# Placing the global keys and queries of a Longformer batch one batch sooner on GpSimd, with the keys in eight copies

## The chip, the core and the metric

The kernel runs on one core of one Trainium2 chip. The metric is the device time of one execution in microseconds (us), lower is better. Times are given as the median of several runs, and one further execution was profiled instruction by instruction. The engines are called PE (TensorE matmul), PEld (its weight load), DVE (VectorE), ACT (ScalarE), POOL (GpSimd) and SP (SyncE, which here only issues DMAs). L12 stands for line 12 of the kernel.

## What is computed

The reference is a Longformer attention, followed by a two-layer block with the activation h + sin²(αh)/α. There are 8 batches, 8 heads, 576 positions and a head size of 64. A position attends to positions at most 32 away, and 8 global positions attend to all and are attended by all:

```python
mask = np.abs(pos[:, None] - pos[None, :]) <= window
mask = mask | is_global[:, None] | is_global[None, :]
attn = softmax(where(mask, q @ k.T / sqrt(D), -1e9))
x = (attn @ v)                       # (8, 8, 576, 64) -> 4608 x 512
h = x @ w_in                         # 512 x 2048
out = (h + sin(alpha * h) ** 2 / (alpha + 1e-9)) @ w_out
```

## The kernel before

**Stages.** Batches are taken one after the other. For each batch b there is an attention stage (`attention`, L712) and then `gemm1(b)` (L947), which computes 16 column tiles of h and applies the activation. `gemm2`, the second product, has no stage of its own: its matmuls (L1033) are dealt out as filler between those of the other stages by `fill`, in numbers that tables at L1076 to L1082 set by hand. The outer loop at L1131 runs `gemm1(b)` and then `phase_a(b + 1, b)`, the attention of the next batch. The schedule is manual: every engine executes its instructions in the order in which the program lists them, and the framework only adds the semaphores that the data need.

**Attention.** Heads are taken in four pairs. For a pair, PE multiplies keys by queries into a PSUM ring (L736, three groups of four key tiles), ACT takes the exponential (L744), DVE multiplies by the mask (L747), and PE multiplies the result by V and by ones (L778, `products`). ACT then makes the inverse of the sums (L804, L807), and DVE the sums over global columns (L788) and the normalised x (L810). The products of a pair are issued behind the first two score groups of the next pair.

**The placed operands.** Keys, queries and V of a batch lie in the tiles `KX`, `QX` and `VX`, each of them twice (index b % 2). In every key tile of 128 partitions and 128 columns, a part holds the 48 keys of a window, and the 8 columns behind them hold the global keys; the same global keys stand in all 12 key tiles of a pair. A batch is brought in by four routes:

- `cast_qk` (L323) casts q and k to bf16 through two DMAs of POOL's queue; `turn_qk` (L333) turns them with two transposing DMAs on SP's queue, after `gemm1` of the batch two before; `place` (L342) copies them into KX and QX on DVE (lines L354 and L347), spread over the attention stage before, or over the end of gemm1(0) and gemm1(1) for batches 1 and 2.
- `load_v` (L385) brings V into VX by four DMAs of POOL's queue for each pair of heads (L390). A pair's DMAs wait until the products of the same pair, two batches before, have read VX.
- `load_vg` (L395) brings V's global rows by eight DMAs of SP's queue (L399).
- `place_globals` (L364) copies the global keys (L368) and queries (L373) into KX and QX on POOL, from the small tiles `kTg` and `qTg`, which hold those of all batches from gemm1(0) on.

**The order on POOL's queue.** At the top of the loop, for b from 1 to 5, POOL gets the casts for b + 2, V's pair 0 for b + 2, `place_globals(b + 1)`, V's pairs 1 to 3 for b + 2, and nothing else until the next b. For b = 6 it gets only `place_globals(7)`. Batch 1's placement is issued inside gemm1(0) (L997). Since V for b + 2 waits for the products of batch b, most of that list runs during attention(b).

**gemm1.** Each of the 16 column tiles takes eight matmuls (L972) into one of three PSUM tiles, zn, zr and zd in turn. ACT takes the sine (L1009), ACT (L1013) or DVE (L1015) the square, and DVE adds the parts (L1020), which frees the PSUM tile. In attention, DVE and ACT also work on a check of the inputs' ranges (`square_x`, L896 to L901, and `square_w`, L870 and L872), which decides at the end whether a general path must run.

The lines of POOL's list in the loop are these:

```python
            cast_qk(b + 2)
            load_v(b + 2, (0,))

            place_globals(b + 1)
            load_v(b + 2, range(1, NHP))
            load_vg(b + 2)
```

Of the kernel before, what the change touches and what calls it, by code (L numbers as in the profile page):

```python
# [18 lines left out]
NG = 8  # L19
KT = 48  # L20
# [227 lines left out]
def kernel(  # L248
# [11 lines left out]
    nc = tc.nc  # L260
    B, H, S, D = q.shape
# [3 lines left out]
    NT12 = S // KT  # L265
    NHP = H // 2
# [27 lines left out]
    KX = [main.tile([P, NHP, NT12, P], DT.bfloat16, name=f"KX{i}") for i in range(2)]  # L294
# [8 lines left out]
    kTg = main.tile([P, NHP, NG, B], DT.bfloat16, name="kTg")  # L303
# [19 lines left out]
    def cast_qk(b):  # L323

        cast[b] = []
        for src, name in ((k, "kd"), (q, "qd")):
            t = dramp.tile([P, H * S * D // P], DT.bfloat16, name=name)
            nc.gpsimd.dma_start(
                out=t[:], in_=src[b].rearrange("h s d -> (h s d)").rearrange("(p f) -> p f", p=P)
            )  # L330
            cast[b].insert(0, t)

    def turn_qk(b):  # L333

        turned[b] = [trp.tile([P, H * HALF], DT.bfloat16, name=name) for name in ("qt", "kt")]
        for i in (1, 0):
            nc.sync.dma_start_transpose(
                out=turned[b][i][:], in_=cast[b][i][:].rearrange("p (r c) -> (p r) c", c=P)
            )
        del cast[b]  # L340
# [22 lines left out]

    def place_globals(b):  # L364

        for t in range(2):
            rows = slice(t * D, (t + 1) * D)
            nc.gpsimd.tensor_copy(  # L368
                out=KX[b % 2][rows, :, :, t * D + KT : t * D + KT + NG],
                in_=kTg[rows, :, None, :, b].to_broadcast([D, NHP, NT12, NG]),  # L370
            )
        for y in range(2):
            nc.gpsimd.tensor_copy(  # L373
                out=globals_of(b, slice(0, P), y),
                in_=qTg[:, :, None, y::2, b].to_broadcast([P, NHP, 7, 4]),
            )

    def globals_of(b, rows, y):

        q0 = QX[b % 2][rows, :, y, PAD : PAD + 4]  # L380
        return bass.AP(
            tensor=q0.tensor, offset=q0.offset, ap=[list(q0.ap[0]), [2 * QROW, NHP], [SEG, 7], [1, 4]]
        )

    def load_v(b, hps=range(NHP)):  # L385
        for hp in hps:
            for t in range(2):
                for y in range(2):
                    r = t * D + y * 24
                    nc.gpsimd.dma_start(  # L390
                        out=VX[b % 2][r : r + 24, hp, :, t * D : t * D + D],
                        in_=v[b, 2 * hp + t].rearrange("(i a y) d -> y a i d", a=24, y=2)[y],
                    )

    def load_vg(b):  # L395
        for h in range(H):
            t = h % 2
            src = VGb[b::B, h * D : (h + 1) * D] if b else VG0[h::H]
            nc.sync.dma_start(  # L399
                out=VX[b % 2][t * D + KT : t * D + KT + NG, h // 2, :, t * D : t * D + D],  # L400
                in_=src[:, None, :].to_broadcast([NG, NT12, D]),
            )
# [35 lines left out]
    for half in range(2):  # L438
        for w, src in ((1, k), (0, q)):
            nc.gpsimd.dma_start(  # L440
                out=nat[w][D * half : D * half + HK],
                in_=src[0, HH * half : HH * half + HH].rearrange("h (i r) d -> (h i) (r d)", r=KT),
# [22 lines left out]
    for t in (gidx8, gp64):  # L465
        nc.vector.memset(t[:].bitcast(DT.int32), 0)
    nc.sync.dma_start(
        out=g64[:],
        in_=bass.AP(tensor=global_idx.tensor, offset=global_idx.offset, ap=[[1, NG], [0, B], [1, 1]]),
# [3 lines left out]
    for t in (0, D):  # L473
        nc.sync.dma_start(out=gp64[t + KT : t + KT + NG], in_=global_idx[:, None])
        nc.sync.dma_start(
            out=gidx8[t + KT : t + KT + NG],
            in_=bass.AP(tensor=global_idx.tensor, offset=global_idx.offset, ap=[[0, NG], [1, NG]]),
# [29 lines left out]
    for i, bits in enumerate((B - 1, D - 1)):  # L507
        nc.vector.tensor_scalar(
            out=rowi[:, i : i + 1], in0=prow[:], scalar1=bits, scalar2=None, op0=ALU.bitwise_and
# [6 lines left out]
        out=cond[:, 0:1], in0=pm, scalar1=float(NH), scalar2=float(1 - KT), op0=ALU.is_ge, op1=ALU.mult  # L516
# [3 lines left out]
        out=kpos[:], in0=pm, scalar=2.0, in1=cond[:, 0:1], op0=ALU.mult, op1=ALU.add  # L520
    )
    nc.vector.scalar_tensor_tensor(
        out=kpos[:], in0=cond[:, 1:2], scalar=float(4095 + KT), in1=kpos[:], op0=ALU.mult, op1=ALU.add
# [4 lines left out]
        out=rowf[0 : NG * B, 4:5], in0=rowf[0 : NG * B, 0:1], scalar=float(S), in1=rowf[0 : NG * B, 3:4], op0=ALU.mult, op1=ALU.add  # L528
# [19 lines left out]
    for name, src in (("k", k), ("q", q), ("v", v)):  # L548
        g0[name] = VG0 if name == "v" else setup.tile([NG * B, D], DT.bfloat16, name="g0" + name)
        nc.gpsimd.indirect_dma_start(  # L550
            out=g0[name][:], out_offset=None, in_=src[0].rearrange("h s d -> (h s) d"),
# [16 lines left out]
        out=band[:], in0=qrel[:], scalar1=float(WIN * WIN) + 0.5, scalar2=None, op0=ALU.is_le  # L568
    )
    for t in (0, D):  # L570
# [4 lines left out]
        out=M2, in_=band[:].rearrange("p e x c -> p e (x c)")[:, None].to_broadcast([P, 6, 2, WCOL])  # L575
# [49 lines left out]
    def place_global_queries(t, copy):  # L625
# [15 lines left out]
        out=first[:], in0=gf[:], scalar1=gpf[:, 0:1], scalar2=None, op0=ALU.not_equal  # L641
# [3 lines left out]
        out=later[:], in0=jrow[:], scalar1=pm, scalar2=float(-KT), op0=ALU.subtract, op1=ALU.is_ge  # L645
# [5 lines left out]
        out=cond[:, 2:3], in0=pm, scalar=float(KT + NG - 1), in1=cond[:, 1:2], op0=ALU.is_le, op1=ALU.mult  # L651
# [5 lines left out]
        out=far[:], in0=qpos[:], scalar1=float(WIN * WIN) + 0.5,  # L657
# [13 lines left out]
    for w, name in ((1, "k"), (0, "q")):  # L671
        pg[w] = both[0:D, 32 + w * 64 : 64 + w * 64].bitcast(DT.bfloat16)
        nc.tensor.transpose(
            out=pg[w][:], in_=g0[name][:], identity=identb[0 : NG * B, 0 : NG * B]
# [272 lines left out]
    def gemm1(b):  # L947
# [35 lines left out]
        for nt in range(NT):  # L983
# [9 lines left out]
            if b == 0 and nt == 11:  # L993

                load_w_out()
                cast_globals_v()
                place_globals(1)  # L997
                load_v(1, (2, 3))
                load_vg(1)
# [91 lines left out]
    def phase_a(b_att, b_moe):  # L1091
        def beside(at):

            if b_moe is None:
                if at == -1:
                    nc.vector.tensor_scalar(out=recipT[:], in0=alphaT[:], scalar1=1e-9, scalar2=None, op0=ALU.add)
                    nc.vector.reciprocal(out=recipT[:], in_=recipT[:])
                if at == 0:
                    second_half()
                    nc.gpsimd.memset(VX[1][:].bitcast(DT.int32), 0)  # L1100
                    nc.gpsimd.memset(QX[1][:].bitcast(DT.int32), 0)
                    nc.gpsimd.memset(KX[1][:].bitcast(DT.int32), 0)
                    turn_qk(1)
                    nc.gpsimd.tensor_copy(out=seen[:], in_=turned[1][1][0:1, 0:1])
                    load_w_in((2, 3))
                    load_v(1, (0, 1))
                    gather(v, gv)
                return
            if at == 0:
                if b_moe == 2:  # L1110
                    column_norms(zn[:, 0, :])
                if b_moe >= 3:
                    token_norms(b_moe - 3, zn[:, 1, :])
            if 0 <= at < 2 and b_moe:
                square_x(b_moe, at)
            if b_att == 1 and at == 0:
                place_rest(1)
                place_rest(0)
            for which, t, y in places_at(b_att, at):
                place(b_att + 1, which, t, y, nc.vector.tensor_copy)  # L1120
            if b_moe == 0 and at == 2:
                turn_qk(2)
            if b_moe == 1 and at in (2, 3):
                square_w(at)

        if b_moe is not None:
            waiting.append(gemm2(b_moe))
        attention(b_att, beside)

    phase_a(0, None)  # L1130
    for b in range(B):  # L1131
        if 0 < b and b + 2 < B:
            cast_qk(b + 2)
            load_v(b + 2, (0,))

            place_globals(b + 1)
            load_v(b + 2, range(1, NHP))
            load_vg(b + 2)
        elif 0 < b < B - 1:
            place_globals(b + 1)  # L1140
        gemm1(b)
        if b + 1 < B:
            if b == 0:
                cast_qk(2)
                load_v(2)
                load_vg(2)
            elif b + 2 < B:
                turn_qk(b + 2)
            phase_a(b + 1, b)
# [46 lines left out]
```

## Time and profile before

| What | us |
|---|---|
| median of 3 runs | 382.2 (379.91 to 382.34) |
| the profiled execution | 381.18 |
| its span, first to last instruction | 379.5 |
| PE, DVE, ACT, POOL busy in it | 342.2, 288.4, 294.3, 133.8 |

The stages follow each other in the profile like this, by the first score matmul and the first gemm1 matmul of each batch:

| batch | attention from | gemm1 from |
|---|---|---|
| 0 | 15.5 | 33.0 |
| 1 | 54.1 | 72.3 |
| 2 | 99.6 | 120.1 |
| 3 | 142.2 | 162.3 |
| 4 | 182.6 | 202.6 |
| 5 | 222.9 | 243.0 |
| 6 | 263.2 | 282.0 |
| 7 | 302.4 | 321.2 |

POOL ran `place_globals` seven times. Its key copies start at 51.1, 86.6, 109.5, 152.5, 192.7, 233.2 and 246.7 us. A line of the profile's order of time gives the start, the time from first to last instruction of a run of equal ones, engine, line, operation, the tiles written and read, the shapes, the number of instructions, and in brackets how long the engine had stood idle before it and what ended that. A line of the wait list gives who waited for whom, the microseconds in total, and how often.

### The profile page before, as it was taken

What the parts mean: (1) busy time and instruction counts of PE and PEld (TensorE: products, weight loads), DVE (VectorE), ACT (ScalarE), POOL (GpSimd) and SP (SyncE); (2) the same over time, 40 slices, a digit from 0 to 9 for tenths busy, and PEclk for the clock granted to TensorE, in tenths of its full rate; (3) what the DMA queues carried; (4) which work ended last, traced back from release to release, by engine and by line L of the source; (5) the groups of instructions that cost most, each with busy time, mean ns of one, the idle gap of its engine ahead of it and who ended that gap; (6) DMA issues with size and microseconds to landing.
All of it is one profiled execution on the core that took longest, in us unless ns stands there. A gap on an engine that the chain in (4) does not pass through costs nothing. (4 is left out here: it accounts for less than half of the span.)

```text
span 379.5 us, 8635 instructions
## 1 busy us (share of the span) xinstructions
PE 342.2 (90%) x3172; PEld 233.3 (61%) x3172; DVE 288.4 (76%) x614; ACT 294.3 (78%) x566; POOL 133.8 (35%) x204
## 2 busy tenths in 40 slices
PE   2679869997998899999989999999999998999893
PEld 2567646764565666676656766666676666776341
DVE  6777897589889887988888888888788876589400
ACT  7789897898889788788878887889888888675111
POOL 7993695559477101840086006720000000000001
PEclk9999999999999999999999999999999999999998
DMA  6999999999999863789069923727111011100221
GB/s 119 119 161 186 155 153 174 147 173 179 182 181 119 137 114 74 91 99 216 28 81 94 204 62 45 75 40 155 42 44 29 0 41 46 29 3 28 57 85 48
DMA packets 103579, 38.08 MB, mean 100 GB/s; under 512 B 94138, under 2 KB 98250, under 8 KB 103082
## 3 DMA queue, kind: packets, MB, share of 16 engines
q0 software_dynamic: 56640, 18.56, 42.4%
q1 hardware_dynamic: 46890, 18.89, 25.1%
q8 instruction: 27, 0.44, 0.5%
q14 instruction: 22, 0.18, 0.1%
HBM read 37.15 MB, written 17.83 MB: 145 GB/s over the span
## 5 line engine op out<-in xcount | busy, mean ns | idle before, releaser
L1033 PE MATMUL zo<-w_out,H 128*128 128x512 bf16 x576 | 153.2, 378 | 0.0
L972 PEld LDWEIGHTS <-w_in 128*128 128x128 bf16 x1024 | 99.2, 97 | 48.4 <-issue 14.8
L390 POOL DMA_DIRECT2D VX<-in_v_dram x128 | 83.7, 663 | 105.7 <-PE zd L778 87.4
L1033 PEld LDWEIGHTS <-H 128*128 128x128 bf16 x576 | 52.0, 97 | 37.3
L744 ACT ACTIVATE E<-ring 128x480 bf16<-128x480 f32 x96 | 54.3, 568 | 24.5 <-PE ring L736 24.0
L972 PE MATMUL zn<-xT,w_in 128*128 128x288 bf16 x376 | 56.2, 285 | 4.7 <-DVE H L1020 2.0
L747 DVE TENSOR_TENSOR E<-E,MASK 128x480 bf16<-128x480 bf16 x96 | 36.6, 411 | 16.2 <-ACT E L744 15.0
L972 PE MATMUL zr<-xT,w_in 128*128 128x288 bf16 x312 | 46.7, 285 | 1.0 <-DVE H L1020 0.6
L972 PE MATMUL zd<-xT,w_in 128*128 128x288 bf16 x312 | 45.4, 285 | 1.6 <-DVE H L1020 1.5
L1020 DVE SCALAR_TENSOR_TENSOR H<-s,recipT,zn 128x576 bf16<-128x576 bf16 x47 | 38.2, 813 | 9.9 <-ACT s L1013 5.5
L1061 POOL DMA_INDIRECT out_dram<-osb,grow x1 | 1.0, 1007 | 125.8 <-SPq L1164 125.8
L1009 ACT ACTIVATE sb<-zn,alphaT 128x576 bf16<-128x576 f32 (+1 forms) x47 | 34.8, 741 | 12.6 <-PE zn L972 9.2
L1013 ACT ACTIVATE s<-sb 128x576 bf16<-128x576 bf16 (+1 forms) x62 | 42.7, 689 | 2.0
L736 PE MATMUL ring<-QX,KX 128*128 128x120 bf16 x384 | 38.3, 226 | 5.6 <-ACT E L744 2.7
L736 PEld LDWEIGHTS <-KX 128*128 128x128 bf16 x384 | 29.1, 102 | 21.7 <-issue 7.6
L1015 DVE TENSOR_TENSOR s<-sb 128x576 bf16<-128x576 bf16 (+1 forms) x66 | 31.4, 475 | 7.7 <-ACT sb L1009 7.4
L1020 DVE SCALAR_TENSOR_TENSOR H<-s,recipT,zd 128x576 bf16<-128x576 bf16 x39 | 31.7, 813 | 6.6 <-ACT s L1013 4.8
L1039 ACT COPY osb<-zo 128x512 f32<-128x512 f32 x36 | 20.8, 578 | 19.7 <-PE zo L1033 19.7
L1020 DVE SCALAR_TENSOR_TENSOR H<-s,recipT,zr 128x576 bf16<-128x576 bf16 x39 | 31.7, 813 | 4.6 <-ACT s L1013 2.5
L1009 ACT ACTIVATE sb<-zd,alphaT 128x576 bf16<-128x576 f32 (+1 forms) x39 | 28.9, 741 | 7.9 <-PE zd L972 5.3
L778 PEld LDWEIGHTS <-VX 128*128 128x128 bf16 x448 | 26.4, 99 | 12.9 <-issue 7.5
L1009 ACT ACTIVATE sb<-zr,alphaT 128x576 bf16<-128x576 f32 (+1 forms) x39 | 28.9, 741 | 4.8 <-PE zr L972 3.5
(160 smaller groups left out, 458.9 us busy)
## 6 DMA issues: line engine op xcount, KB each, us to landing
VX<-in_v_dram POOLq DMA_DIRECT2D x128, 36.0 KB, 3.6
kd<-in_k_dram POOLq DMA_DIRECT2D x7, 576.0 KB, 6.6
qd<-in_q_dram POOLq DMA_DIRECT2D x7, 576.0 KB, 8.9
w_in<-in_moe_w_in_dram POOLq DMA_DIRECT2D x4, 512.0 KB
w_out<-in_moe_w_out_dram POOLq DMA_DIRECT2D x4, 512.0 KB, 8.9
out_dram<-osb SPq DMA_DIRECT2D x8, 256.0 KB
out_dram<-osb SPq DMA_DIRECT2D x8, 224.0 KB
out_dram<-osb SPq DMA_DIRECT2D x8, 192.0 KB
```

What stands on the lines that cost most here:

```text
L390: nc.gpsimd.dma_start(out=VX[b % 2][r : r + 24, hp, :, t * D : t * D + D], in_=v[b, 2 * hp + t].rearrange("(i a y) d -> y a i d", a=24, y= ...
L736: nc.tensor.matmul(out=ps[:, e * WCOL : (e + 1) * WCOL], lhsT=kx[:, hp, i, :], rhs=qx[:, hp, :, s0 : s0 + 60], start=True, stop=True, skip ...
L744: nc.scalar.activation(out=Eg, in_=ps[:, 0 : 4 * WCOL], func=AF.Exp, scale=scale, accum_out=EA[:, n : n + 1])
L747: nc.vector.tensor_tensor(out=Eg, in0=Eg, in1=MASK[:, 4 * g : 4 * g + 4, :].rearrange("p i c -> p (i c)"), op=ALU.mult,)
L778: nc.tensor.matmul(out=out_t[:, half, :, a - half * CUT : z - half * CUT], lhsT=OB[:] if key else VXb[:, hp, i, :], rhs=E[:, i, :, a - s0 ...
L972: nc.tensor.matmul(out=h[e][:, 0:HALF], lhsT=lhsT, rhs=xT[:, c, e, :], start=(c == 0), stop=(c == CT - 1), skip_group_check=True,)
L1009: nc.scalar.activation(out=sb[:, es, 0:W], in_=h[:, :, 0:W], func=AF.Sin, scale=alphaT[:, nt : nt + 1])
L1013: nc.scalar.activation(out=s2[:, :, 0:W], in_=sb[:, :, 0:W], func=AF.Square)
L1015: nc.vector.tensor_tensor(out=s2[:, :, 0:W], in0=sb[:, :, 0:W], in1=sb[:, :, 0:W], op=ALU.mult)
L1020: nc.vector.scalar_tensor_tensor(out=dst.rearrange("p (e c) -> p e c", e=2)[:, es], in0=s2[:, es, lo:hi], scalar=recipT[:, nt : nt + 1], i ...
L1033: nc.tensor.matmul(out=ops[:], lhsT=H2[:, nt, blk * P : (blk + 1) * P], rhs=w_out[:, nt, :], start=(nt == 0), stop=(nt == NT - 1),)
L1039: nc.scalar.copy(out=osb[:], in_=ops[:])
```

## The change

`place_globals` copies the keys pair of heads by pair of heads: eight copies of 64 partitions and 96 elements in place of two of 64 partitions and 384 elements. The two query copies stay as they are.

In the loop, for b from 1 to 5, POOL now gets the placement for b + 2 (not b + 1), and it stands between V's pair 2 and V's pair 3 for b + 2 (not between pairs 0 and 1). With b = 1 the placement for batch 2 stays where it was, so that this turn has two. The separate placement with b = 6 goes away. Batch 1's placement inside gemm1(0) stays, with the eight copies.

```diff
     def place_globals(b):
 
-        for t in range(2):
-            rows = slice(t * D, (t + 1) * D)
-            nc.gpsimd.tensor_copy(
-                out=KX[b % 2][rows, :, :, t * D + KT : t * D + KT + NG],
-                in_=kTg[rows, :, None, :, b].to_broadcast([D, NHP, NT12, NG]),
-            )
+        for hp in range(NHP):
+            for t in range(2):
+                rows = slice(t * D, (t + 1) * D)
+                nc.gpsimd.tensor_copy(
+                    out=KX[b % 2][rows, hp, :, t * D + KT : t * D + KT + NG],
+                    in_=kTg[rows, hp, None, :, b].to_broadcast([D, NT12, NG]),
+                )
         for y in range(2):
             nc.gpsimd.tensor_copy(
...
         if 0 < b and b + 2 < B:
             cast_qk(b + 2)
             load_v(b + 2, (0,))
-
-            place_globals(b + 1)
-            load_v(b + 2, range(1, NHP))
+            if b == 1:
+                place_globals(2)
+            load_v(b + 2, (1, 2))
+            place_globals(b + 2)
+            load_v(b + 2, (3,))
             load_vg(b + 2)
-        elif 0 < b < B - 1:
-            place_globals(b + 1)
         gemm1(b)
```

## The prediction

> **What bounds the kernel now.** I read the page's busy times first, then a table of the attention stretches, then the order of time on DVE and on POOL in the same stretch, and last the waits.
>
> ```profile
> PE 342.2 (90%) x3172; PEld 233.3 (61%) x3172; DVE 288.4 (76%) x614; ACT 294.3 (78%) x566; POOL 133.8 (35%) x204
> ```
>
> PE is the bound over the whole span, but it isn't full everywhere. The table by windows has one row per attention stretch, for batches 2, 3, 4, 5 and 6, each from its first score matmul to the next gemm1. Columns: us, then busy time of PE, PEld, DVE, ACT, POOL, granted clock, DMA share, GB/s.
>
> ```profile
> 99.56:120.13 20.57, 19.24 (x213) 12.52 (x213) 16.43 (x34) 18.31 (x41) 11.34 (x17) 1.00 1.29 182
> 142.20:162.31 20.11, 19.26 (x228) 12.89 (x228) 17.00 (x40) 16.20 (x41) 10.83 (x16) 1.00 0.55 84
> 182.60:202.61 20.01, 18.99 (x214) 12.60 (x213) 16.87 (x37) 16.21 (x41) 11.01 (x16) 1.00 0.51 63
> 222.93:243.02 20.09, 19.14 (x213) 12.60 (x213) 16.79 (x37) 16.16 (x41) 10.84 (x16) 1.00 0.45 60
> 263.19:282.03 18.84, 18.83 (x214) 12.61 (x213) 15.44 (x37) 15.76 (x41) 0.00 (x0) 1.00 0.24 54
> ```
>
> Batches 4, 5 and 6 do the same PE and DVE work (213 or 214 matmuls, 37 DVE instructions). Batch 6 has nothing on POOL, fills PE, and is 1.17 to 1.25 us shorter. It is the control for this change. The next two views are DVE in order of time, in batch 3 (with POOL's copies) and in batch 6 (without):
>
> ```profile
> 152.26 1.79 DVE L899 TENSOR_TENSOR SQ<-SQ 128x1152 bf16<-128x1152 bf16 x2
> 154.09 0.86 DVE L901 TENSOR_TENSOR SR<-SQ 128x288 bf16<-128x288 bf16 x1
> 154.96 0.58 DVE L354 COPY KX<-kt 64x1152 bf16<-64x1152 bf16 x1
> 155.56 1.11 DVE L747 TENSOR_TENSOR E<-E,MASK 128x480 bf16<-128x480 bf16 x3
> ```
>
> ```profile
> 272.97 1.24 DVE L899 TENSOR_TENSOR SQ<-SQ 128x1152 bf16<-128x1152 bf16 x2
> 274.25 0.31 DVE L901 TENSOR_TENSOR SR<-SQ 128x288 bf16<-128x288 bf16 x1
> 274.57 0.45 DVE L354 COPY KX<-kt 64x1152 bf16<-64x1152 bf16 x1
> 275.05 1.05 DVE L747 TENSOR_TENSOR E<-E,MASK 128x480 bf16<-128x480 bf16 x3
> ```
>
> The same four lines take 4.41 us and 3.13 us. What runs beside them in batch 3 is on POOL:
>
> ```profile
> 149.91 2.63 POOL L390 DMA_DIRECT2D VX<-in_v_dram  x4 [25.63 <-PE zd L778]
> 152.54 2.24 POOL L368 COPY KX<-kTg 64x384 bf16<-64x384 bf16 x2
> 154.84 0.93 POOL L373 COPY QX<-qTg 128x112 bf16<-128x112 bf16 x2
> 155.72 2.59 POOL L390 DMA_DIRECT2D VX<-in_v_dram  x4
> 159.38 2.55 POOL L390 DMA_DIRECT2D VX<-in_v_dram  x4 [1.07 <-PE zd L778]
> 162.78 0.64 POOL L390 DMA_DIRECT2D VX<-in_v_dram  x1 [0.84 <-PE zd L778]
> ```
>
> The key copies hold up each bf16 DVE instruction that meets one: the second L899 takes 1006 ns against 457 alone, L901 856 against 307. DVE is in front here: the masks L747 come late, and PE stands 0.84 us before the products at 157.66, put down to DVE xT L810 (1.01 in batch 4, 0.84 in 5, 0.48 in 2).
>
> **Part 1, taken out of the middle of attention(2) to (5).** Batch 6 against the others, less what lies ahead of the copies: from the start of L899 to gemm1 it is 10.05 (batch 3), 10.22 (4), 10.06 (5) and 9.06 us (6), so 1.0 + 1.15 + 1.0 = 3.15. In attention(2) DVE gives back 1.4 us (749+996, 873, 617 and 583 ns against 749+457, 307, 406 and 406), but ACT's R ends at 112.63 and L810 ran at 113.46, so 0.8 at most and at least PE's own 0.48: I take 0.6. Gain 3.75 (bounds: PE idle alone 3.2; the whole windows 1.27+1.17+1.25+0.8 = 4.5). The copies for batch 7, at 246.68 in gemm1(5), also leave; L1015 took 840 ns there against 452, but PE did not stand: nothing.
>
> **Part 2, the short copies.** Over 14 each, an undisturbed key copy (384 elements a partition) took 841 ns, a query copy (112) 371: 1.73 ns an element and 178 ns fixed, so 344 ns for 96 elements, an estimate. Bounds: 210 (a quarter of 841) and 612 (a disturbed query copy). With the 0.05 us between copies, eight take 3.15 us where two took 1.8: each placement is 1.3 us longer on POOL.
>
> What a short one does to DVE decides the case. Beside query copies, L354 took 577 against 453 (+0.12), L747 474 against 406 (+0.07), L347 422 and 392 against 300 (+0.12, +0.09); beside key copies the same kinds lost 0.4 to 0.59. I take 0.13 per bf16 DVE instruction, since 96 elements are near 112; bounds 0.07 and the whole 0.34. L1020, which reads PSUM, took 812 to 817 beside copies and 814 elsewhere: nothing.
>
> The rule that speaks against me is in the Trainium skill, SBUF — State Buffer, section "SBUF: two separate sides": the port pair that GpSimd and VectorE share is an exclusive lock for the whole instruction. By it each meeting would cost up to a whole copy. The trace agrees that it is a lock, but L354 at 154.96 met a query copy that ended at 155.21 and lost 0.12, not 0.25. By the rule the sum is that of the second rival.
>
> **Part 3, where the copies now lie.** V's third pair still waits for products(2); its four issues end at 161.93 in batch 3's old times. The copies wait for nothing: the last scores read KX and QX at 158.5 to 158.9, before. They run from 161.93 to about 165.9 (3.15 + 0.77). Up to 164.0 DVE does L788, L810, L859 and L860, on PSUM or tiny; then comes the opening of gemm1:
>
> ```profile
> 164.00 0.93 DVE L347 COPY QX<-qt 64x1152 bf16<-64x1152 bf16 x2
> 165.00 0.46 DVE L1015 TENSOR_TENSOR s<-sb 128x576 bf16<-128x576 bf16 x1
> 165.57 0.81 DVE L1020 SCALAR_TENSOR_TENSOR H<-s,recipT,zn 128x576 bf16<-128x576 bf16 x1
> 166.43 1.14 PE L972 MATMUL zn<-xT,w_in 128*128 128x288 bf16 x8
> ```
>
> This chain has no slack: L1020 ends at 166.38 and frees zn for the matmul at 166.43. Three bf16 instructions by 0.13 is 0.4 in batch 3. In batch 4 L1020 waited 0.46 for PE (L1033), so 0.1; in batch 5 L1015 waited 0.22 for ACT, so 0.2; in batch 2 four L347 follow, PE already stands 1.12 for L1020, and part of the copies is over by then, so 0.5. Cost 1.2.
>
> V's last pair starts when the copies are done, near 165.9 instead of 162.78, and the two casts behind it are 1.1 to 2.2 us later. The cast at 166.41 is transposed on SP at 208.23: 40 us of cover. That pair of V is read one batch later, and load_vg on SP writes other rows: nothing.
>
> **Part 4, placements 1 and 2, which stay put.** Batch 1's copies start at 51.15. The wait list says who needs them:
>
> ```profile
> PEld L736 <- POOL QX L373: 2.0, 1, 2.0
> ```
>
> They end at 53.82 and would end near 55.1. The scores at 54.14 move 1.0 to 1.3, but ACT loads its table until 55.42 before it can take them, and L347 (883 ns at 51.41) is freed sooner: cost 0.2 (0 to 0.9). At 86.60, for batch 2, L872 took 1870 ns against 1226 and PE stood 1.47 before L972 at 91.21 for DVE: 0.13 in place of 0.64 gives 0.3 back (0 to 0.6). The eight V issues behind are 1.3 later, then batch 3's copies fall at about 97 to 101, at the end of gemm1(1): L347, L1015 and L747 lose 0.13 each; PE has filler: 0.2 (0 to 0.5). POOL stood 6.95 us before 106.87, which covers the 5.2 us that its queue is behind by then.
>
> **The sum.** 3.75 + 0.3 - 1.2 - 0.2 - 0.2 = 2.45 faster. The profiled execution took 381.18 us (379.5 span and 1.7 around it): 378.7. It lies 1.0 under the median of the runs, 382.2; the four executions shown average 381.4, and from that I say **379.0**.
>
> **The rivals.** *Free passage:* the copies slip under DVE's PSUM instructions and part 3 costs nothing, while part 1 gives the whole windows: 4.5 + 0.3 - 0.1 = 4.7, so 376.7. For it: five of the ten fit before 164.0. Against: the rest do not.
> *Whole copies:* each meeting costs 0.34: 1.4 + 1.0 + 0.55 + 0.8 = 3.75 at the openings, 0.4 and 0.5 in part 4, no 0.3 back: 0.9 slower, 382.3. For it: 0.59 at 51.41. Against: the query copies' 0.07 to 0.12.
> *The opening of gemm1 blocked (slower):* if DVE's PSUM readers stop for copies too, nine instructions by 0.34 less 0.5 of idle, 2.5 us a batch, four batches: 10 - 3.75 + 0.9, so 388.5. It decides from 1.0 us a batch (3.75 over four). Against: L1020 does not stop; L810 beside a copy is not in this trace.
> That the copies are not moved out of attention would need a wait on them; the scores end too early for one.
>
> **How the numbers follow.** Forecast 0.54 (377.9 to 380.3), free passage 0.22, whole copies 0.18, blocked opening 0.06. The range 376.6 to 382.6 leaves out half of free passage, the blocked opening and a part of whole copies. One per cent, about what can be told from no change, is 3.8 us: faster by more means under 378.4, which is free passage and a fifth of the forecast, 0.33; slower by more, over 386.0, is the blocked opening, 0.05; within, 0.62.
>
> **What would show it.** Right: L901 near 307 ns in attention(2) to (5), these stretches near 18.9 to 19.1, key copies near 350 ns, L347 and L1015 at the openings some 0.13 longer, PE's wait for L1020 there up to 0.5. Wrong: L810 longer, L347 by 0.3 or more, scores of batch 1 after 55.5, or a wait of PE that comes up elsewhere in the attention.

## The result, and the profile after

The changed kernel took 378.69 us (median of 9 runs, 376.65 to 391.58), the kernel before 381.25 beside it (9 runs, 379.65 to 382.34). The ratio is 0.9916, 95% interval 0.9888 to 0.9944. Two later comparisons of the same two kernels gave 0.9927 (0.9886 to 0.9968) and 0.9937 (0.9903 to 0.9972). 379.0 had been predicted. The ratios leave out executions that took over 1.5% more than the fastest of their kernel, in these three comparisons 13 of the 34 of the changed kernel and 2 of the 55 of the kernel before. Over all executions the means are 381.6 and 381.1, so that on average the change gained nothing: the 3 us that an ordinary execution gains are lost again in the long ones. The two long ones that were profiled hold a wait in attention(5), which has a section of its own below.

The first profiled execution is one of these, so the lines here come from a later profile of the changed kernel: 377.98 us, span 376.3, against 381.18 and 379.5 before. The line numbers are higher by one behind L364 (L899 is now L900). The page's busy times:

```profile
PE 337.6 (90%) x3124; PEld 232.3 (62%) x3172; DVE 282.4 (75%) x614; ACT 294.2 (78%) x566; POOL 139.8 (37%) x246
```

DVE lost 6.0 us of work with the same 614 instructions, and POOL has 42 instructions and 6.0 us more. The table by windows has batches 2 to 6 again, from first score matmul to first gemm1 matmul (us, then PE, PEld, DVE, ACT, POOL, granted clock, DMA share, GB/s):

```profile
98.72:118.41 19.69, 18.98 (x208) 12.55 (x212) 14.90 (x33) 17.43 (x40) 10.65 (x19) 1.00 1.23 174
141.53:160.65 19.12, 18.90 (x224) 12.91 (x228) 15.81 (x40) 16.21 (x41) 8.10 (x13) 1.00 0.64 101
181.14:199.98 18.84, 18.67 (x210) 12.60 (x213) 15.51 (x37) 16.21 (x41) 8.10 (x13) 1.00 0.56 74
220.45:239.54 19.09, 18.83 (x210) 12.59 (x213) 15.65 (x37) 16.16 (x41) 8.09 (x13) 1.00 0.68 108
259.68:278.52 18.84, 18.67 (x210) 12.60 (x213) 15.44 (x37) 15.77 (x41) 0.00 (x0) 1.00 0.27 59
```

Batch 4 now takes the 18.84 of batch 6, the control; batches 3 and 5 come within 0.28. Batch 2 went from 20.57 to 19.69. The first gap closes where the prediction put it. DVE in attention(3), the same four lines as before:

```profile
151.60 1.24 DVE L900 TENSOR_TENSOR SQ<-SQ 128x1152 bf16<-128x1152 bf16 x2
152.88 0.31 DVE L902 TENSOR_TENSOR SR<-SQ 128x288 bf16<-128x288 bf16 x1
153.20 0.45 DVE L354 COPY KX<-kt 64x1152 bf16<-64x1152 bf16 x1
153.68 1.05 DVE L748 TENSOR_TENSOR E<-E,MASK 128x480 bf16<-128x480 bf16 x3
```

4.41 us are now 3.13, the figure of the control to the hundredth. POOL's order of time shows where the copies went:

```profile
157.72 2.55 POOL L391 DMA_DIRECT2D VX<-in_v_dram  x4 [1.71 <-PE zd L779]
160.27 3.42 POOL L369 COPY KX<-kTg 64x96 bf16<-64x96 bf16 x8
163.75 0.81 POOL L374 COPY QX<-qTg 128x112 bf16<-128x112 bf16 x2
164.51 0.66 POOL L391 DMA_DIRECT2D VX<-in_v_dram  x1
165.73 1.91 POOL L391 DMA_DIRECT2D VX<-in_v_dram  x3 [0.56 <-issue]
167.63 0.53 POOL L328 DMA_DIRECT2D kd<-in_k_dram  x1
```

They start 0.38 us ahead of gemm1(3), at 160.65, and end 3.9 behind it; V's last pair and the casts stand behind them. The opening of gemm1(3), first DVE, then PE:

```profile
162.41 1.07 DVE L347 COPY QX<-qt 64x1152 bf16<-64x1152 bf16 x2
163.51 0.49 DVE L1016 TENSOR_TENSOR s<-sb 128x576 bf16<-128x576 bf16 x1
164.11 0.81 DVE L1021 SCALAR_TENSOR_TENSOR H<-s,recipT,zn 128x576 bf16<-128x576 bf16 x1
```

```profile
164.97 1.14 PE L973 MATMUL zn<-xT,w_in 128*128 128x288 bf16 x8
```

Two L347 lost 0.14 together and L1016 0.03; L1021 lost nothing. The matmul that needs zn comes 4.32 us after gemm1's first where it had come 4.12 after: 0.20 lost.

The sum over the stages, changed less before: start to gemm1(1) +0.25, gemm1(1) -1.08, attention(2) -0.88, gemm1(2) +1.05, attention(3) to (5) -1.00, -1.17 and -1.01, gemm1(3) to (5) +0.20, +0.15 and -0.03, the rest +0.31. That is -3.2, the difference of the spans.

### The profile page after: what moved, and what is told of

It reads as the page before. It is cut to its first block, busy times and chain, and to the rows that moved or that the text cites. A ratio compares the mean times of both kernels' runs of the same rounds, so it can differ in the third digit from the quotient of the medians.

```text
span 382.0 us, 8629 instructions
## 1 busy us (share of the span) xinstructions
PE 338.2 (89%) x3124; PEld 232.6 (61%) x3172; DVE 282.0 (74%) x614; ACT 293.7 (77%) x566; POOL 140.4 (37%) x246
## 5 line engine op out<-in xcount | busy, mean ns | idle before, releaser
L1034 PE MATMUL zo<-w_out,H 128*128 128x512 bf16 x528 | 143.1, 380 | 2.1 <-issue 0.2
L748 DVE TENSOR_TENSOR E<-E,MASK 128x480 bf16<-128x480 bf16 x96 | 35.7, 404 | 14.9 <-ACT E L745 13.7
L1021 DVE SCALAR_TENSOR_TENSOR H<-s,recipT,zn 128x576 bf16<-128x576 bf16 x47 | 38.2, 813 | 10.5 <-ACT s L1014 6.0
L737 PE MATMUL ring<-QX,KX 128*128 128x120 bf16 x384 | 37.4, 222 | 8.0 <-ACT E L745 3.8
L1021 DVE SCALAR_TENSOR_TENSOR H<-s,recipT,zd 128x576 bf16<-128x576 bf16 x39 | 31.7, 813 | 6.5 <-ACT s L1014 4.8
L1016 DVE TENSOR_TENSOR s<-sb 128x576 bf16<-128x576 bf16 (+1 forms) x66 | 30.6, 464 | 7.2 <-ACT sb L1010 6.9
L1021 DVE SCALAR_TENSOR_TENSOR H<-s,recipT,zr 128x576 bf16<-128x576 bf16 x39 | 31.7, 813 | 4.5 <-ACT s L1014 2.4
```

The lines of the kernel that those rows point to most:

```text
L737: nc.tensor.matmul(out=ps[:, e * WCOL : (e + 1) * WCOL], lhsT=kx[:, hp, i, :], rhs=qx[:, hp, :, s0 : s0 + 60], start=True, stop=True, skip ...
L748: nc.vector.tensor_tensor(out=Eg, in0=Eg, in1=MASK[:, 4 * g : 4 * g + 4, :].rearrange("p i c -> p (i c)"), op=ALU.mult,)
L1016: nc.vector.tensor_tensor(out=s2[:, :, 0:W], in0=sb[:, :, 0:W], in1=sb[:, :, 0:W], op=ALU.mult)
L1021: nc.vector.scalar_tensor_tensor(out=dst.rearrange("p (e c) -> p e c", e=2)[:, es], in0=s2[:, es, lo:hi], scalar=recipT[:, nt : nt + 1], i ...
L1034: nc.tensor.matmul(out=ops[:], lhsT=H2[:, nt, blk * P : (blk + 1) * P], rhs=w_out[:, nt, :], start=(nt == 0), stop=(nt == NT - 1),)
```

## The experiments

The theory (A) was the prediction's own: what a copy costs is the hold-up of each bf16 DVE instruction that meets it, and the shorter copy holds less. The rivals: the place is what counts and the length nothing (B); at the new place the copies must be short, or the openings of gemm1 pay for them (C); POOL's placements still cost more than that wherever they stand (D). The stages of the profiles, in us:

| kernel | attention 2 | gemm1 2 | attn. 3 | gemm1 3 | attn. 4 | gemm1 4 | attn. 5 |
|---|---|---|---|---|---|---|---|
| before | 20.57 | 22.07 | 20.12 | 20.29 | 20.01 | 20.32 | 20.10 |
| changed (later profile) | 19.69 | 23.12 | 19.12 | 20.49 | 18.84 | 20.47 | 19.09 |
| short_only | 20.27 | 22.43 | 19.34 | 20.29 | 19.09 | 20.31 | 19.33 |
| move_long | 19.67 | 29.84 | 19.12 | 20.35 | 18.84 | 20.38 | 19.09 |
| no_place | 19.66 | 26.72 | 19.12 | 20.29 | 18.84 | 20.32 | 19.09 |
| four_copies | 20.53 | 22.11 | 20.10 | 20.29 | 19.83 | 20.32 | 20.06 |
| late | 19.68 | 23.05 | 19.12 | 20.34 | 18.84 | 20.32 | 19.08 |
| sixteen_copies | 20.14 | 22.42 | 19.12 | 20.29 | 18.83 | 20.31 | 41.63 |

**The short copies alone, at the old place** (short_only).

```diff
-        for t in range(2):
-            rows = slice(t * D, (t + 1) * D)
-            ... KX[b % 2][rows, :, :, ...]
+        for hp in range(NHP):
+            for t in range(2):
+                rows = slice(t * D, (t + 1) * D)
+                ... KX[b % 2][rows, hp, :, ...]
```

> The eight short key copies at the old place, nothing moved. Theory A (a DVE instruction loses what the copy in front of it holds, 0.05 to 0.13 us for a short one): L899, L901, L354 and L747 in attention(3) to (5) lose at most 0.5 us together where they lost 1.28, so these stretches shrink from 20.0 to 20.1 to 19.2 to 19.5 us, gemm1(1) gains the same 1.1 us as the changed kernel, and the whole is 2 to 3.5 us faster than before, about as fast as the changed kernel. Rival B (the place is what counts): ten copies still stand in the middle of attention and DVE loses their total time, so attention(3) to (5) stay at 19.9 us or more and the whole is within 1.2 us of before.

Measured: 378.47 (376.97 to 390.6), ratio 0.9931 (0.9893 to 0.997). Attention(3) to (5) keep 0.22 to 0.25 us of the copies' cost each and the openings pay nothing. B asked for 19.9 or more there and falls. DVE in its attention(4), where all eight copies still lie beside these lines:

```profile
189.94 1.27 DVE L900 TENSOR_TENSOR SQ<-SQ 128x1152 bf16<-128x1152 bf16 x2
191.24 0.34 DVE L902 TENSOR_TENSOR SR<-SQ 128x288 bf16<-128x288 bf16 x1
191.59 0.54 DVE L354 COPY KX<-kt 64x1152 bf16<-64x1152 bf16 x1
192.17 1.43 DVE L748 TENSOR_TENSOR E<-E,MASK 128x480 bf16<-128x480 bf16 x3
```

L902 loses 0.03, L354 0.09, three L748 0.38 together in the order of time (0.06, 0.15 and 0.16 by themselves; up to 0.19 in attention(2)).

**The new place alone, with the two long copies** (move_long).

```diff
-        for hp in range(NHP):
-            for t in range(2):
-                ... KX[b % 2][rows, hp, :, ...]
+        for t in range(2):
+            ... KX[b % 2][rows, :, :, ...]
```

> The new place with the two long key copies. Theory A: they run from the end of V's pair 2 for 1.8 us, which ends under L788, L810, L859 and L860, none of which a copy holds up, so the openings of gemm1(3) to (5) cost 0.2 us each or less, attention(3) to (5) are 18.8 to 18.9 us as in the changed kernel, but gemm1(1) loses its 1.1 us again (L872 near 1870 ns); whole 0.5 to 2 us faster than before. Rival C (the short copies are needed at the new place): L347 and L1015 at the openings lose 0.4 to 0.6 us each, gemm1(3) to (5) grow by 1.0 to 1.5 us each, and the whole is as slow as before or slower by up to 3 us.

Measured: 385.8 (377.92 to 394.0), ratio 0.9948 (0.9902 to 0.9994), with 8 of 13 executions long (383.8 or more). The openings took 20.35 and 20.38, no more than those of the changed kernel, so C falls too: two long copies are over after 1.8 us, before most of the DVE instructions that they could meet. Its gemm1(1) took 28.18 against 26.20, since the long copies of batches 2 and 3 lie there, and in gemm1(2) ACT waited 5.0 us for output stores that stood on SP's queue behind a transpose of 16.8 us. Length and place are two ways to the same gain, and the second adds little to the first.

**Both, once more** (after_again), beside the two before.

> The changed kernel as it is, for a second profile and for a comparison in the same session. All theories expect 2 to 3 us less than before (ratio 0.992 to 0.995). Attention(5), which in the first profile of the changed kernel held a stretch at half the TensorE clock, should here be near 18.85 us like attention(4) (18.84), against 20.10 before; L901 307 ns in attention(2) to (5).

Measured: 380.26 (376.41 to 392.76), ratio 0.9927 (0.9886 to 0.9968), against 0.9931 for the short copies alone. Attention(3) and (4) took 19.12 and 18.84 again, gemm1(3) and (4) 20.43 and 20.45. Attention(5) had been expected near 18.85 and took 34.53, a miss (see the wait below).

**No placements for batches 2 to 7** (no_place).

```diff
-            if b == 1:
-                place_globals(2)
...
-            place_globals(b + 2)
```

> The changed kernel without the placements for batches 2 to 7: their global keys and queries are not placed, so a part of the attention is left out. It bounds what all of POOL's placements cost from batch 2 on. Theory A: attention(3) to (5) 18.84 us, gemm1(3) and (4) back from 20.47 and 20.50 to 20.3 us, gemm1(1) no more than 0.3 us under the changed kernel; whole 0.5 to 1.2 us faster than the changed kernel. Rival D (short copies still cost DVE much, only elsewhere): 2 us or more faster than the changed kernel.

Measured: 377.61 (7 runs), ratio 0.9885 (0.9832 to 0.9938). Attention(3) to (5) are those of the changed kernel to the hundredth; only the openings give back 0.20 and 0.15. D asked for 2 us or more. The intervals of this ratio and of the changed kernel's 0.9927 are too wide to decide that, but the stages do: with batch 1's placement kept, 0.3 to 0.4 us are all that the copies still cost from gemm1(3) on. The profiled execution (380.36) lost 3.6 us in gemm1(2), where ACT waited for output stores as in move_long.

**Halves instead of quarters** (four_copies): the keys in four copies of 192 elements, at the old place.

```diff
-        for t in range(2):
+        for p in range(2):
+            for t in range(2):
+                rows, hps = slice(t * D, (t + 1) * D), slice(2 * p, 2 * p + 2)
+                ... KX[b % 2][rows, hps, :, ...]
```

> The kernel before, with the keys in four copies of 192 elements a partition at the old place. Theory A (DVE loses what is left of the copy that it meets): the loss lies between that of the two copies of 384 and the eight of 96, so L901 in attention(3) to (5) takes 450 to 650 ns (856 and about 360) and attention(4) 19.3 to 19.7 us (20.01 and 19.09). Rival E (a meeting costs DVE a fixed time, and the number of meetings counts): attention(4) under 19.1 us.

Measured: 380.3, before 381.04, ratio 0.9983 (0.9958 to 1.0007). Attention(4) took 19.83, and 19.3 to 19.7 had been expected: a miss, though L902 is in the expected 450 to 650 ns. DVE there:

```profile
191.25 1.45 DVE L900 TENSOR_TENSOR SQ<-SQ 128x1152 bf16<-128x1152 bf16 x2
192.74 0.53 DVE L902 TENSOR_TENSOR SR<-SQ 128x288 bf16<-128x288 bf16 x1
193.28 0.72 DVE L354 COPY KX<-kt 64x1152 bf16<-64x1152 bf16 x1
194.03 1.63 DVE L748 TENSOR_TENSOR E<-E,MASK 128x480 bf16<-128x480 bf16 x3
```

Each instruction that meets a copy loses 0.17 to 0.27 where it lost 0.55 to a long one, but six meet one where two or three did. The four lines take 4.41 us (4.57 in the same batch before, 3.66 with eight copies).

**Copies half as long as the change's** (sixteen_copies): sixteen copies of 48 elements, at the old place.

```diff
+        for hp in range(NHP):
+            for t in range(2):
+                for z in range(2):
+                    rows, its = slice(t * D, (t + 1) * D), slice(6 * z, 6 * z + 6)
+                    ... KX[b % 2][rows, hp, its, ...]
```

> The kernel before, with the keys in sixteen copies of 48 elements a partition at the old place. From the runs so far the loss of a DVE instruction that meets a copy is about 0.55 us at 384 elements, 0.20 at 192, 0.09 at 112 and 0.03 to 0.09 at 96, which is 1.73 ns an element less 0.11 us. Theory A2 (that law: a part of some 0.11 us of each copy is free): at 48 elements nothing is lost at the key copies, L901 is 307 to 315 ns and attention(4) 18.84 to 18.95 us (19.09 with eight copies), though POOL is busy for 5 us. Rival E (a fixed loss for each meeting, so twice the copies cost more): 19.2 us or more.

Measured: 400.97 (399.31 to 403.12), ratio 1.0557 (1.0504 to 1.061), the largest miss of the study. Yet attention(3) and (4) are those of the changed kernel, 19.12 and 18.83, although every copy lies in them. The squares of the check lose nothing beside copies of 48 elements (457 and 308 ns; the lines are L901 and L903 in this kernel). But the law that had been expected isn't the whole: of each three masks, two still lose 0.07, without a loss to the stage. One of them in attention(4), and the copy that it meets:

```profile
193.47 0.47 DVE L749 TENSOR_TENSOR E<-E,MASK 128x480 bf16<-128x480 bf16 x1
```

```profile
193.23 0.44 POOL L370 COPY KX<-kTg 64x48 bf16<-64x48 bf16 x1
```

When the mask starts, 0.20 us of the copy are left, and it takes 0.47 where it takes 0.40 alone. What counts is this rest, not the number of elements: over the 14 profiles, a bf16 DVE instruction (squares, masks, L347, L354, L1015, L872) that starts while a copy runs takes longer by the rest of that copy less 0.135 us, and by nothing where the rest is shorter. Of 346 such starts, 341 fit to 0.02 us. The 1.73 ns an element less 0.11 us give 0.06 for a mask that meets a copy of 96 elements, and two of three lost 0.15 to 0.16.

The 22 us are lost in attention(5), in one wait, below.

**The placement behind V's last pair** (late).

```diff
-            load_v(b + 2, (1, 2))
+            load_v(b + 2, range(1, NHP))
             place_globals(b + 2)
-            load_v(b + 2, (3,))
```

> The changed kernel with the placement for b + 2 behind V's last pair, so that it runs some 2.6 us later, inside gemm1. Theory A: the two L347 are past by then and only some L1015 meet a copy at 0.05 to 0.09 us, with PE in front: gemm1(3) and (4) 20.29 to 20.36 us (20.43 to 20.50 in the changed kernel), attention(3) and (4) 19.12 and 18.84 as there; whole 0.2 to 0.6 us faster than the changed kernel. Rival F (gemm1 has no slack for DVE anywhere): gemm1(3) and (4) at 20.45 us or more.

Measured: 377.13 (376.29 to 377.83), ratio 0.9898 (0.9865 to 0.9932). The copies start at 164.96, behind the opening, whose L347 take 0.93 us together as in the kernel before:

```profile
162.56 0.93 DVE L347 COPY QX<-qt 64x1152 bf16<-64x1152 bf16 x2
```

gemm1(3) and (4) take 20.34 and 20.32. So 0.15 us an opening was the price of the place, as A has it.

**Where attention(2)'s gain went** (before_nosq, changed_nosq): both kernels without two of the four squares of `square_w`, one execution each.

```diff
-            if b_moe == 1 and at in (2, 3):
-                square_w(at)
```

> The kernel before without the squares of w_in that ACT and DVE make in attention(2) (L870 and L872 there, a part of the check of the ranges). Alone it gives the baseline for the next run: attention(2) and gemm1(2) together were 42.64 us and should lose 1.5 to 3 us.

> The changed kernel without the squares of w_in that ACT and DVE make in attention(2) (a part of the check of the ranges). Theory A (batch 2 gained nothing because ACT's squares set its pace, not DVE): attention(2) and gemm1(2) together are now 0.6 to 1.1 us shorter than in the run of the kernel before without them, as in batches 3 and 4. Rival G (the four L347 at the opening of gemm1(2) give it all back): the two are within 0.2 us of each other.

Measured: attention(2) and gemm1(2) together take 40.94 and 40.40, a gain of 0.54; with the squares 42.64 and 42.81, none. The result lies between the two theories (0.6 to 1.1, and 0.2 or less). Without the squares attention(2) gains 0.73 and gemm1(2) loses 0.19 (21.50 to 21.69), with them 0.88 and 1.05: the squares take most of the gain. The 0.19 are near what L347 and L1016 lose to copies at that opening (0.2 in the changed kernel). The whole times, 377.45 and 377.73, don't show it, since the second execution took 2.8 us longer in gemm1(0) and attention(1), a stretch that lasts 38.2 to 41.7 us in the 14 profiles. PE's first matmuls on zr in gemm1(2) show it, first before, then the changed kernel, both with the squares:

```profile
121.37 0.90 PE L972 MATMUL zr<-xT,w_in 128*128 128x288 bf16 x6 [0.34 <-DVE GS L788]
```

```profile
120.53 0.90 PE L973 MATMUL zr<-xT,w_in 128*128 128x288 bf16 x6 [1.22 <-DVE GS L789]
```

And DVE's last square in the changed kernel says why:

```profile
119.12 1.22 DVE L873 TENSOR_TENSOR W<-W,SQ 128x2048 bf16<-128x2048 bf16 x1 [1.51 <-ACT SQ L871]
```

ACT's square (1.91 us at 117.18) comes in its queue ahead of the inverse of the last pair. DVE, now early, waits 1.51 for it (0.63 before), and PE stands 0.88 longer behind DVE. PE had gained 0.88 in the stage.

**The best place again, and with the shortest copies** (late_again, changed_third, late_sixteen). The last has the edits of late and sixteen_copies together.

> The changed kernel with the placement behind V's last pair, once more beside the changed kernel in one session. By the stages of the profiles it should be 0.2 to 0.6 us faster than the changed kernel (gemm1(3) 20.34 against 20.43 to 20.47, gemm1(4) 20.32 against 20.45 to 20.50), which is less than the runs can tell apart; the rival is no difference at all, with the gain of 0.1 us a stage given back elsewhere.

> The changed kernel beside the run before it. All theories: 2.5 to 3.5 us faster than before; gemm1(3) 20.43 to 20.47 us and gemm1(4) 20.45 to 20.50.

> Sixteen key copies of 48 elements a partition, and the placement behind V's last pair. Two questions. First, the law of the loss (1.73 ns an element less 0.11 us): gemm1(3) and (4) 20.29 to 20.34 us and attention(4) 18.84, as with eight copies at this place, so at full TensorE clock the whole lies within 0.5 us of that run (376.6 to 377.1). Second, the half clock that all executions with sixteen copies at the old place showed for some 20 us of attention(5): if it comes with the sixteen copies, attention(5) is 30 us or more here too and the whole 390 or more; if it came from how the stages fell in that kernel, attention(5) is 19.09 us.

Measured: late 376.57 (375.89 to 377.64), ratio 0.9896 (0.9861 to 0.9931); changed kernel 381.81 (376.73 to 388.21), 0.9937 (0.9903 to 0.9972); late with sixteen copies 378.28 (376.57 to 380.85), 0.995 (0.9924 to 0.9977). The changed kernel's median is above that of the kernel before (380.69) this time, since half of its 12 executions were long; 2.5 to 3.5 us faster had been expected. Late is the best version found. Its ratio isn't clearly under that of the changed kernel, but none of its 12 executions in the two comparisons took over 377.83, where the changed kernel's reach 388 to 393. Sixteen copies gain nothing at a place where eight no longer disturb, and miss the expected 376.6 to 377.1: gemm1(3) and (4) are at 20.29 and 20.31, but the scores of batch 1 wait 4.1 us for the sixteen copies, where they wait 1.6 in late. Attention(5) took 19.08 at full clock, so the stretch at half clock doesn't come with sixteen copies as such.

## A wait that comes with the change

In the changed kernel's first profile, its second and that of sixteen_copies, attention(5) took 25.72, 34.53 and 41.63 us. The wait lists of that stage name the same waiter, DVE's placement of batch 6's keys. First profile, second, sixteen_copies (us in total, times, longest):

```profile
DVE KX L354 <- DMA kt<-kd: 6.1, 1, 6.1
```

```profile
DVE KX L354 <- DMA kt<-kd: 15.3, 1, 15.3
```

```profile
DVE KX L354 <- DMA kt<-kd: 22.0, 1, 22.0
```

Later in the chain ACT and PE stand behind DVE. The half clock that shows in such an execution comes after the wait. In sixteen_copies PE's last matmul ends at 226.1, and the granted clock falls to a half at 230.45, when PE has stood for 4.3 us. In the table by windows, the clock is the third number from the right:

```profile
226.00:232.00 6.00, 0.14 (x1) 0.00 (x0) 0.00 (x0) 0.37 (x2) 0.00 (x0) 0.87 0.89 51
232.00:244.00 12.00, 0.00 (x0) 0.00 (x0) 0.00 (x0) 0.00 (x0) 0.00 (x0) 0.50 1.44 40
```

The Trainium skill, TensorE: Matmul & The Clock Gate, Part 1, has the same order: the clock is gated after about 3.4 us without work.

What the DMAs did is in the order of time on SP and POOL, around 205 us. sixteen_copies:

```profile
205.11 12.63 SPq L337 DMA_TRANSPOSE kt<-kd  x1
217.84 26.29 SPq L337 DMA_TRANSPOSE qt<-qd  x1
```

```profile
205.89 0.53 POOL L328 DMA_DIRECT2D kd<-in_k_dram  x1
```

late:

```profile
205.44 2.08 SPq L337 DMA_TRANSPOSE kt<-kd  x1
207.62 8.64 SPq L337 DMA_TRANSPOSE qt<-qd  x1
```

```profile
207.00 0.53 POOL L328 DMA_DIRECT2D kd<-in_k_dram  x1
```

The transposes are those of batch 6, the cast that of batch 7. They don't need each other, but where they run at the same time, each can be slow: in sixteen_copies the casts land 35 and 38 us after their issue, in late 6.6 and 8.8. DVE's placement starts when the second transpose ends (244.13 and 244.25 in sixteen_copies), though it reads only what the first one writes; why isn't shown. In this stage, over all profiles, the time for both transposes goes with the distance between the first of them and the first cast:

| kernel | first cast after first transpose | both transposes |
|---|---|---|
| before, before_nosq, four_copies, no_place | -2.7 to -2.6 | 9.3, 9.5, 9.3, 9.7 |
| short_only | -1.8 | 10.3 |
| move_long | -0.5 | 13.0 |
| sixteen_copies | +0.8 | 39.0 |
| changed, three profiles, and changed_nosq | +0.9 to +1.0 | 23.5, 32.6, 17.6, 16.9 |
| late, late_again | +1.6 | 10.8, 10.1 |
| late_sixteen | +2.6 | 12.8 |

DVE's placement comes some 17 us after the first transpose, so the third profile of the changed kernel just hides it (0.2 us of wait). The distance isn't the whole rule: around 96 us, for the batches three earlier, a cast 3.8 us after the first transpose went with 20.3 us (move_long). All this is read from the traces and wasn't tried by a run that moves the casts alone. Whether the two slow each other, and why, stays open. So does which wait the long executions hold that were not profiled: 3 of 12 of short_only, whose casts come before the transposes, and 2 of 17 of the kernel before (388.61 and 389.23, in the last comparison with the changed kernel).

## Why the prediction was right, and where not

**Part 1, the middle of attention(2) to (5): right.** 3.15 was predicted for batches 3 to 5, 3.18 measured, and batch 6 was the right control. For batch 2 the step took 0.6 and the stage gave 0.88.

**Part 2, the short copies: right in size, not in kind.** 3.13 us for eight undisturbed at 51.4, where 3.15 had been worked out. A meeting was put at 0.13 with bounds of 0.07 and 0.34. At the openings of gemm1(3) to (5) L347 and L1016 lost 0.04 to 0.09, and at the old place most lost 0.03 to 0.09, two masks of three 0.15 to 0.19. The price was taken from the number of elements; what set it is the rest of the copy at the start, less 0.135. L354 at 154.96, held against the rule, fits too: 0.256 of the query copy were left, and it lost 0.12. The rule weighed there (the Trainium skill, SBUF — State Buffer, "SBUF: two separate sides": locked for the whole instruction) is thus borne out but for 0.135 us at the copy's end, and what these are stays open. The second rival's sum charged a whole copy for each meeting, where a DVE instruction meets only the rest of one.

**Part 3, the openings: right in sum by luck, wrong in its terms.** 1.2 was predicted, and gemm1(2) to (5) lost 1.37. But batches 3, 4 and 5 paid 0.20, 0.15 and -0.03 where 0.4, 0.1 and 0.2 stood, and batch 2 paid 1.05 where 0.5 stood. The term for batch 2 counted L347 meeting copies, and without the squares gemm1(2) lost 0.19; the term missed that PE and DVE would wait there for ACT's square.

**Part 3, V's last pair and the casts: the step that failed.** It said that the casts come 1.1 to 2.2 us later, that they have 40 us of cover, and so: nothing. They came 2.9 us later in gemm1(3) and 3.4 in gemm1(4). The cover is for their own transposes. Batch 7's cast moved against batch 6's transposes: before it was issued 3.0 us after the start of gemm1(4), changed 6.4 after, and the transposes at 5.6 and 5.4. In the three profiles DVE waited 6.1, 15.3 and 0.2 us for those transposes, and PE stood behind it: the prediction's own sign of being wrong, a wait of PE that comes up elsewhere in the attention. That the distance to the cast is the cause is likely by the table above, but not shown.

**Part 4, placements 1 and 2: size wrong.** 0.2 was to be lost at the first. PE's first scores of batch 1 wait for POOL:

```profile
PE ring L737 <- POOL QX L374: 2.0, 1, 2.0
```

The weight load waited as long before (2.0). From gemm1(0)'s last matmul to gemm1(1)'s first it took 18.7 to 20.0 us in the eight profiles with eight copies and 19.3 to 19.9 in the three with two, so that no loss can be told. At the second, 0.3 gained and 0.2 lost were predicted; gemm1(1) lost 1.08 us of its 27.28. L873 went from 1870 to 1250 ns, as predicted, and the step missed L1015 ahead of it, 1024 ns before and 452 now, in the same chain to zd: PE's waits for the line that frees the PSUM tiles (L1020, now L1021) fell from 2.0 to 1.1 us in that stage. Not all of this is the change's: with the same two long copies there, before_nosq took 26.69 for gemm1(1), so the gain is 0.5 to 1.1.

**The number: luck in part.** An ordinary execution gained 3.2 us, where 2.45 had been summed up: 0.3 more in the middle of the attentions and 0.4 to 1.0 more in gemm1(1), less 0.2 at the openings and 0.3 behind the start of attention(6). The median of 378.69 comes so close to 379.0 because three of the nine executions were long, and the one of them that was profiled holds a wait that the sum put at nothing; the other six have a median of 377.6.

**The rivals.** *Blocked opening* fell: L811 took 747 to 759 ns beside copies and 748 to 759 away from them. *Whole copies* fell with 0.03 to 0.19 a meeting. *Free passage* (376.7) came close in batch 5, where the opening cost nothing, and its time is what late reaches, by copies that run behind the opening.

## What to carry to other kernels

Where POOL's copies hold up DVE, cut them until little of one is left when the next DVE instruction starts, and measure in the stage: halving gained nothing that can be told (0.9983, 0.9958 to 1.0007), because more instructions met a copy, and quartering gained nearly all. Look at the long executions too before calling a change a gain: here they took back on average what the ordinary ones gained. When a change shifts one queue's DMAs against another's, look at what runs beside them, not only at who waits for their data. A gain ends at the next engine in line: most of the 0.88 us of attention(2) went to a square on ACT that had been hidden.

## What the runs showed of the hardware

A bf16 DVE instruction with its operands in SBUF that starts while a copy runs on POOL takes longer by the rest of that copy less 0.135 us. Three of the 341 starts that fit: L901 before, at 154.09, 0.69 us of a copy of 384 elements left, 0.55 lost; L902 in short_only, at 191.24, 0.17 of one of 96 left, 0.03 lost; L749 in sixteen_copies, at 193.47, 0.20 of one of 48 left, 0.07 lost. A copy that starts during a DVE instruction waits in turn: in sixteen_copies those beside L354 in attention(4) took 0.52 and 0.54 us, undisturbed ones 0.25 to 0.27. DVE instructions that read PSUM lost nothing beside any copy (in changed_third L811 747 to 759 ns, L1021 806 to 815). Around 205 us two transposes on SP's queue took 9 to 13 us in eight kernels, and 17 to 39 us in those where a cast on POOL's queue was issued 0.8 to 1.0 us after the first of them.
